# A linear-attention block and a SoLU block in one kernel: conversion order, the second group's keys, fetch order, and the place of state reads

## Chip, core and metric

The kernel runs on one core of a Trainium2 chip. The metric is its device time in microseconds, as the median of several runs. Before the change it is 368.37 us (three runs, 367.83 to 369.05).

## What is computed

Gated linear attention over 4 batches, 8 heads, 768 tokens and 48 channels, followed by a feed-forward block on the 3072 tokens of 384 channels (8 heads side by side):

```python
for t in range(S):
    state = alpha[:, :, t, :, None] * state + np.einsum('bhd,bhe->bhde', k[:, :, t], v[:, :, t])
    y[:, :, t] = np.einsum('bhd,bhde->bhe', q[:, :, t], state)
...
h = x @ w_in                                  # 384 -> 1024
solu = h * softmax(h)
ln = (solu - mean) / sqrt(var + 1e-06) * g_ln
return ln @ w_out                             # 1024 -> 384
```

The two weight matrices come as 64-bit floats; everything else is float32.

## The kernel before, in words

The 768 tokens are cut into G = 6 groups of 128 tokens in each of B = 4 batches, so a group is 512 tokens (T4). For each group there are two jobs. The attention job turns alpha, k and q so that channels lie on partitions, makes running products of alpha by a backward and a forward scan on VectorE (`scan_back`, `scan_on`, line 204), multiplies keys and queries by them, forms scores inside the chunk (`scores`, line 278), masks them (line 289), reads the carried state (`read_state`) and the values (`read_values`, both line 333) into x, and updates the state (`next_state`, line 371). The feed-forward job does eight blocks f of 128 hidden channels: `up_mm` (line 394, three products of 128 x 128 by 128 x 512), the exponential on ScalarE (line 408), the product h * e on VectorE (line 409), its square on ScalarE (line 412), then `down` (line 507, eight products of 128 x 128 by 128 x 385 for each of four token blocks), and `finish`, which normalises with sums that `array_sums` and `token_sums` gather on TensorE. Every float32 product is two matmul instructions in the trace, each with its own weight load.

The order of instructions on each engine is written out by hand; each engine works through its own queue in order, and a queue waits where its next instruction needs something. DMAs are issued from SyncE's queue (SP), in order too.

The stretch that the change touches most is the start. Group 0's attention is done first. Then group 0's up loop (`for f in range(FC)`, line 747) runs while the 64-bit weights arrive and are turned into float32 in eight pieces: pieces 0 to 3 are `w_in` (two blocks f each), pieces 4 to 7 are `w_out`. Each piece takes five VectorE steps, `bit(i, k)` with k = 0 to 4 (lines 616, 620, 624, 628, 630; 128 x 768 elements each, and each step needs the one before it). `fetch` brings raw pieces into slots of `room`, a buffer of six slots whose slots are also used for the hidden activations u; a fetch into a slot waits until the piece in it was converted and examined (`in_range`, ScalarE, lines 598 and 601). Pieces of `w_out` are then scaled by `g_ln` on ScalarE (`scaled`, line 637).

Behind the up loop (lines 773 to 844) stand, by hand: group 1's keys and queries, turned by TensorE against the identity (`turned`, line 164), the four `down` blocks of group 0, sums, the mean of `w_out` (`mean`, line 651 and 658), scans, `keys_back` (line 303, which turns the finished keys back for the state update), scores and masks of group 1, and group 1's state and value reads. From the third group on, keys, queries and alpha are turned by VectorE in 32 x 32 blocks (`firsts`, `lasts`, lines 179 and 182), and keys and queries are multiplied on GpSimd.

Last comes the main loop over g = 1 to 5 (line 922): group g's up blocks, with the down blocks of the group before between them, and group g + 1's attention in pieces that two tables name by step s: `first` for g = 1 and `usual` for g = 2, 3, 4. `head` comes ahead of the up block of step s, `behind` after it, `middle` ahead of the down block, `tail` after it. `attend` (line 863) turns the names into work. There, `lasts` stands for the queries' last 16 channels: turning, copying the decay's end (`ends_of_decay`), multiplying, and eight DMAs to `q64` (`move_lasts`); `firsts` is the same for the first 32 channels with four DMAs (`move_firsts`). `decay` multiplies the state on GpSimd by the ends that arrive in `q64`.

PSUM is handed out by tag: `ps_h` has two buffers for h, `ps_o` two for down, and `ps_a` has four single banks, a0 to a3, which scores, reads, turns and sums share.

## Time and profile before

| what | us |
|---|---|
| median of 3 runs | 368.37 |
| the profiled execution, its own time | 367.97 |
| its span, first to last instruction | 366.2 |
| PE busy in the span | 357.8 |
| VectorE busy | 245.0 |
| ScalarE busy | 146.4 |
| GpSimd busy | 132.2 |

By stretch (us of busy time):

| stretch | PE | VectorE | ScalarE | GpSimd | DMA share |
|---|---|---|---|---|---|
| 0 to 30 | 26.88 | 20.78 | 15.61 | 9.54 | 0.92 |
| 30 to 40 | 10.00 | 9.83 | 7.54 | 0.00 | 0.77 |
| 40 to 50 | 10.00 | 8.90 | 8.24 | 0.00 | 1.11 |
| 50 to 60 | 10.00 | 9.76 | 7.14 | 0.00 | 1.05 |
| 60 to 70 | 10.00 | 9.69 | 5.37 | 0.00 | 0.23 |
| 70 to 80 | 9.85 | 8.17 | 6.34 | 0.47 | 0.32 |
| 110 to 120 | 9.74 | 8.85 | 4.91 | 9.11 | 0.62 |
| 320 to 366 | 41.34 | 15.37 | 9.18 | 10.34 | 0.09 |

A line of the timeline gives the start in us, how long the run of like instructions took, engine, source line, operation, the tiles written and read, shapes and count; what stands in brackets is idle time before it and what ended that. Times in the trace count from the start of the span. A matmul's end is modelled and includes the way through the array, so the rate is read from starts.

### The profile page before, as it was taken

Reading aid. Unit: us, or ns where it says so; the run is one execution under the profiler, and the core shown is the slowest. Engines: PE = TensorE matmul, PEld = TensorE weight load, DVE = VectorE, ACT = ScalarE, POOL = GpSimd, SP = SyncE. Lnnn points to the kernel's source line nnn. Section 1 sums busy time; section 2 is a strip of 40 time slices with the busy share of each in tenths; the row PEclk is TensorE's granted clock in tenths of the full one; section 3 lists DMA queues with packets and bytes.
Section 4 is the critical chain, followed back from the end, with each engine's and each line's share of the span. In section 5 each row is a group of like instructions: output and inputs, shape, how many; then the busy total and the mean of one; then the engine's idle time right before and its main releaser. Section 6 shows DMA issues by size and latency. Waiting matters only on the chain. (4 is left out here: it accounts for less than half of the span.)

```text
span 366.2 us, 10036 instructions
## 1 busy us (share of the span) xinstructions
PE 357.8 (98%) x4341; PEld 215.0 (59%) x4341; DVE 245.0 (67%) x375; ACT 146.4 (40%) x260; POOL 132.2 (36%) x129
## 2 busy tenths in 40 slices
PE   8899999999999999999999999999999999999994
PEld 8784355666755566566575456475556565555552
DVE  0999989979998797936675935766946314345420
ACT  3647878182645262252521252431241132222110
POOL 7020000004449963774133764232773121233300
PEclk9999999999999999999999999999999999999999
DMA  9995995326196409463035354004041000000011
GB/s 180 183 338 152 204 309 124 88 67 159 50 234 141 109 21 180 85 152 94 21 92 112 83 121 126 3 25 88 21 107 55 0 25 0 24 21 22 23 47 51
DMA packets 72871, 36.06 MB, mean 98 GB/s; under 512 B 48232, under 2 KB 70000, under 8 KB 72816
## 3 DMA queue, kind: packets, MB, share of 16 engines
q1 hardware_dynamic: 71792, 34.39, 39.8%
q10 hardware_dynamic: 1024, 0.92, 0.8%
q8 instruction: 36, 0.59, 0.7%
q14 instruction: 19, 0.16, 0.2%
HBM read 25.30 MB, written 4.72 MB: 82 GB/s over the span
## 5 line engine op out<-in xcount | busy, mean ns | idle before, releaser
L507 PE MATMUL o<-w_out,room 128*128 128x385 f32 x384 | 134.0, 492 | 0.0
L394 PE MATMUL h<-x,w_in 128*128 128x512 f32 x288 | 131.7, 597 | 0.5 <-DVE g_col L642 0.5
L507 PEld LDWEIGHTS o<-w_out,room 128*128 128x128 f32 x384 | 71.0, 189 | 54.7 <-issue 13.1
L394 PEld LDWEIGHTS h<-x,w_in 128*128 128x128 f32 x288 | 53.2, 189 | 58.6 <-issue 48.5
L409 DVE TENSOR_TENSOR room<-h,e 128x512 f32<-128x512 f32 x40 | 27.5, 689 | 72.9 <-ACT e L408 72.9
L408 ACT ACTIVATE e<-h 128x512 f32<-128x512 f32 x40 | 24.0, 599 | 100.2 <-PE h L394 100.2
L427 POOL TENSOR_TENSOR p<-p,e 128x512 f32<-128x512 f32 x30 | 43.7, 1458 | 20.0 <-ACT e L408 19.9
L412 ACT ACTIVATE u<-room 128x512 f32<-128x512 f32 x40 | 25.2, 630 | 38.3 <-DVE room L409 38.3
L546 POOL TENSOR_TENSOR r<-sums,mhalf 128x1 f32<-128x1 f32 x20 | 14.8, 741 | 69.7 <-DVE sums L537 69.4
L289 DVE TENSOR_TENSOR sT<-a,mask 128x512 f32<-128x512 f32 x43 | 26.7, 681 | 8.0 <-PE a L278 7.9
L204 DVE TENSOR_TENSOR_SCAN hT<-aT,unit 128x516 f32<-128x516 f32 x18 | 24.4, 1399 | 7.6 <-ACT aT L703 7.5
L204 DVE TENSOR_TENSOR_SCAN aT<-aT,seed 128x516 f32<-128x516 f32 x18 | 27.4, 1551 | 0.2
L225 POOL TENSOR_TENSOR kT<-kT,hT 128x1024 f32<-128x1024 f32 (+1 forms) x8 | 14.2, 1800 | 32.7 <-DVE kT L179 32.7
L427 DVE TENSOR_TENSOR p<-p,u 128x512 f32<-128x512 f32 x30 | 22.5, 749 | 5.1 <-ACT u L412 5.1
L278 PEld LDWEIGHTS a<-qv,kT 32*128 32x128 f32 x704 | 21.4, 186 | 7.0 <-issue 2.6
L278 PE MATMUL a<-qv,kT 32*128 32x128 f32 x704 | 23.9, 278 | 0.4 <-POOL qv L253 0.3
L212 POOL COPY fend<-hT 128x12 f32<-128x12 f32 x6 | 3.1, 509 | 55.9 <-DVE hT L204 55.9
L333 PE MATMUL y<-sT,vn 128*32 128x128 f32 x768 | 22.6, 273 | 0.2 <-DVE sT L289 0.2
L333 PEld LDWEIGHTS y<-sT,vn 128*32 128x32 f32 x768 | 20.7, 110 | 1.6 <-issue 1.0
L196 ACT ACTIVATE sq<-an,mone 128x1536 uint8<-128x1536 f32 x12 | 18.9, 1572 | 0.2
L548 ACT ACTIVATE o_sb<-o,r 128x384 f32<-128x384 f32 x16 | 9.3, 582 | 18.5 <-POOL r L546 18.5
L261 POOL TENSOR_TENSOR state<-state,lot 128x384 f32<-128x384 f32 x10 | 8.8, 903 | 13.1 <-DMA lot<-qv 13.1
(148 smaller groups left out, 374.3 us busy)
## 6 DMA issues: line engine op xcount, KB each, us to landing
vn<-in_v_dram SPq DMA_DIRECT2D x24, 192.0 KB, 4.7
an<-in_alpha_dram SPq DMA_DIRECT2D x20, 192.0 KB, 4.1
out_dram<-o_sb SPq DMA_DIRECT2D x20, 192.0 KB, 1.9
room<-in_moe_w_out_dram SPq DMA_DIRECT2D x8, 384.0 KB, 5.5
kn<-in_k_dram SPq DMA_DIRECT2D x16, 192.0 KB, 5.6
qn<-in_q_dram SPq DMA_DIRECT2D x16, 192.0 KB, 4.1
lot<-qe SPq DMA_DIRECT2D x40, 64.5 KB, 2.1
lot<-qv SPq DMA_DIRECT2D x20, 129.0 KB, 2.4
```

What stands on the lines that cost most here:

```text
L196: nc.scalar.activation(out=sq, in_=x, func=AF.Relu, scale=sign, bias=mone, accum_out=over[:, g, i : i + 1])
L204: nc.vector.tensor_tensor_scan(out=o, data0=a, data1=s, initial=1.0, op0=ALU.mult, op1=ALU.add)
L278: nc.tensor.matmul(a[b][:, i], lhsT=kT[quarter(b), kb], rhs=qv[quarter(b), qb, 0:P], start=not last and not i, stop=bool(last), tile_posit ...
L289: nc.vector.tensor_tensor(out=sT[:, b, half * NP : half * NP + NP], in0=a[b], in1=mask[:, None, :].to_broadcast([P, NP, P]), op=ALU.mult,)
L333: nc.tensor.matmul(y_bank(b)[quarter(r), a], lhsT=lhsT, rhs=rhs, start=(b, r) not in begun, stop=stop, tile_position=(row, 32 * r), skip_g ...
L394: nc.tensor.matmul(h, lhsT=w_in[:, a, f * P : (f + 1) * P], rhs=d["x"][:, a].rearrange("p b t -> p (b t)"), start=(a == 0), stop=(a == KC ...
L408: nc.scalar.activation(out=e, in_=h, func=AF.Exp)
L409: nc.vector.tensor_tensor(out=u, in0=h, in1=e, op=ALU.mult)
L412: nc.scalar.activation(out=u2, in_=u, func=AF.Square)
L427: eng.tensor_tensor(out=p, in0=d[0][i] if f == 1 else p, in1=d[f][i], op=ALU.add)
L507: nc.tensor.matmul(d["o"][:, 0 : DM + 1], lhsT=u_of(g, f)[:, b * P : b * P + P], rhs=w_out[:, f], start=(f == 0), stop=(f == FC - 1), skip ...
L546: nc.gpsimd.tensor_tensor(out=r, in0=s[:, 3:4], in1=mhalf, op=ALU.pow)
```

## The change

What it does, in the order of the diff's parts:

- The copies of the decay's end for group 2 (the third) are done by ScalarE and not by GpSimd.
- In group 0, up blocks f = 2 to 7 are computed in two halves of 256 columns; the first thirty down steps (blocks n = 0 to 2 and f = 0 to 5 of n = 3) in two halves of 192 and 193 columns.
- The last three small operations of `token_sums(0)` are put off until after the second half of group 1's masks.
- A fetch of two pieces lays them in one slot each, and not interleaved.
- Piece 0 is converted in two halves (one up block each); from piece 1 on, the steps of one piece and of the next alternate. As many steps as before come ahead of the up loop; their distribution over f differs.
- k of group 1 is loaded in the plain layout, and VectorE turns it (`keys_T(1)`); TensorE's turn of it and ScalarE's copy of its ends fall away. The load of k for group 2 stands behind that turn.
- Fetches of pieces 5 and 6 go to f = 1 and f = 3, ahead of alpha's load, which moves from f = 0 to f = 3.
- Behind the up loop, `down(0, 0)` precedes the array sums, and all of q's turns stand together ahead of the mean. PSUM tags are dealt out anew. Scans and key multiplications alternate differently.
- For group 2, q is turned ahead of the main loop, and two of the three forward scans move from there into steps 0 and 1; `lasts` moves from step 2 to step 1.
- In groups 4 and 5 (the last two), the first half of the state read moves from step 6 to step 7, directly ahead of the second half.

```diff
-    def ends_of_decay():
-        nc.gpsimd.tensor_copy(out=qe[:, :, P:SW], in_=h4[:, H:NB, 1:2])
-        nc.gpsimd.tensor_copy(out=qv[:, 0:H, P:SW], in_=h4[:, 0:H, 1:2])
+    def ends_of_decay(copy=nc.gpsimd.tensor_copy):
+        copy(out=qe[:, :, P:SW], in_=h4[:, H:NB, 1:2])
+        copy(out=qv[:, 0:H, P:SW], in_=h4[:, 0:H, 1:2])
...
+        w = T4 if g or f < 2 else T4 // 2
         for a in range(KC):
-            nc.tensor.matmul(
-                h, lhsT=w_in[:, a, f * P : (f + 1) * P], rhs=d["x"][:, a].rearrange("p b t -> p (b t)"),
-                start=(a == 0), stop=(a == KC - 1),
-            )
+            x = d["x"][:, a].rearrange("p b t -> p (b t)")
+            for c in range(0, T4, w):
+                nc.tensor.matmul(
+                    h[:, c : c + w], lhsT=w_in[:, a, f * P : (f + 1) * P], rhs=x[:, c : c + w],
+                    start=not a and not c, stop=(a == KC - 1), skip_group_check=True,
+                )
...
         tt = work.tile([P, B, 2, 32], FP, name="cols")
         nc.vector.transpose(out=tt.rearrange("p b i t -> p (b i t)"), in_=t.rearrange("p b i t -> p (b i t)"))
         s = sums[:, g * B : g * B + B]
-        nc.vector.tensor_copy(out=s[:, :, 1:3], in_=tt[:, :, :, 0])
-        sq = small.tile([P, B], FP, name="sq")
...
-        d["s"] = small.tile([P, B], FP, name="s")
-        nc.vector.scalar_tensor_tensor(
...
+        def rest():
+            nc.vector.tensor_copy(out=s[:, :, 1:3], in_=tt[:, :, :, 0])
...
+            nc.vector.tensor_tensor(out=sq, in0=s[:, :, 1], in1=s[:, :, 1], op=ALU.mult)
+            d["s"] = small.tile([P, B], FP, name="s")
...
+        if g:
+            rest()
+        else:
+            d["rest"] = rest
...
+            w = DM // 2 if n * FC + f < 30 else DM + 1
+            for c in range(0, DM, w):
+                e = DM + 1 if c + w >= DM else c + w
+                nc.tensor.matmul(
+                    d["o"][:, c:e], lhsT=u_of(g, f)[:, b * P : b * P + P], rhs=w_out[:, f, c:e], start=not f and not c,
+                    stop=(f == FC - 1), skip_group_check=True,
+                )
...
-        raw = room[:, 1536 * slot : 1536 * (slot + n)].bitcast(U32).rearrange("p (c f w) -> p c f w", f=w, w=2)
+        raw = room[:, 1536 * slot : 1536 * (slot + n)].bitcast(U32)
+        raw = raw.rearrange("p (m c f w) -> p c m f w", m=n, f=w // n, w=2)
...
-                nc.sync.dma_start(out=raw[rows, c].rearrange("p f w -> p (f w)"), in_=src.bitcast(U32))
+                nc.sync.dma_start(
+                    out=raw[rows, c].rearrange("p m f w -> p m (f w)"),
+                    in_=src.bitcast(U32).rearrange("p (m x) -> p m x", m=n),
+                )
...
-            raws[i + m] = raw[:, :, w // n * m : w // n * (m + 1)]
+            raws[i + m] = raw[:, :, m]
...
+    def bit(i, k, part=None):
...
+        dst = place(i)
         top, low = made[i]
+        if part is not None:
+            lo, hi, top, low, dst = (x[:, :, P * part : P * part + P] for x in (lo, hi, top, low, dst))
...
-        m = ps_h.tile([P, 512], FP, tag="h", name="sums")[:, 0:DM]
+        m = ps_a.tile([P, 512], FP, tag="a3", name="sums")[:, 0:DM]
...
-    bits(0)
+    bits((0, k, part) for k, part in ((0, 0), (0, 1), (1, 0), (1, 1), (2, 0), (2, 1), (3, 0), (4, 0), (3, 1), (4, 1)))
     read_values(0)
     gains()
     keys_back(0)
     in_range(0)
-    bits(1)
...
+    steps = [(1, 0), (1, 1)]
+    for i in range(1, 8):
+        steps += [(i, 2), (i + 1, 0), (i, 3), (i + 1, 1), (i, 4)]
+    steps = [x for x in steps if x[0] < 8]
+
+    def convert(n):
+        bits(steps[:n])
+        del steps[:n]
+
+    convert(5)
+    checks = {0: [(2, 0)], 1: [(2, 1)], 2: [(3, 0)], 3: [(3, 1)], 4: [(4, 0), (4, 1)], 5: [(1, 0), (1, 1)]}
...
+        if f == FC - 1:
+            scaled(5)
...
     for f in range(FC):
         up_mm(0, f)
         if f == 4:
...
         up_act(0, f, lambda: check(f))
-        for _ in range((4, 2, 3, 3, 3, 3, 3, 9)[f]):
...
+        convert((5, 2, 3, 2, 5, 4, 2, 7)[f])
         if f == 0:
             next_state(0)
             fetch(4, 3)
-            load_first(k, kn, 1)
+            load(k, kn, 1)
             load_first(q, qn, 1)
+        elif f == 1:
+            fetch(5, 1)
+        elif f == 3:
+            fetch(6, 2)
             load(alpha, an, 1)
-        elif f == 2:
-            ends_k = ends_of(kn, "e")
-        elif f == 3:
-            fetch(5, 1)
-            fetch(6, 2)
             ends_q = ends_of(qn, "u2")
         elif f == 5:
             fetch(7, 3)
             load_v(1)
         elif f == 6:
             scaled(4)
-    tk = three("tp_k", [(ps_a, "a2"), (ps_a, "a3"), (ps_h, "h")])
-    turned(kn, ends_k, tk)
+    down(0, 0)
+    array_sums(0, 1)
+    scaled(6)
+    scaled(7)
+    down(1, 0)
+    keys_T(1)
     load(k, kn, 2)
-    array_sums(0, 1)
-    scaled(5)
-    down(0, 0)
-    scaled(6)
+    token_sums(0)
     alpha_over(1)
-    token_sums(0)
     alpha_T(1)
     load(alpha, an, 2)
-    down(1, 0)
-    scaled(7)
-    tq = three("tp_q", [(ps_a, "a0"), (ps_a, "a1")])
-    turned(qn, ends_q, tq, range(H))
-    for i in range(3):
-        scan_back(1, i)
-        part = slice(NP * i, NP * i + NP)
-        nc.vector.tensor_tensor(out=kT[:, part], in0=tk[i], in1=hk[:, part], op=ALU.mult)
+    tq = three("tp_q", [(ps_a, "a0"), (ps_h, "h"), (ps_a, "a2")])
+    turned(qn, ends_q, tq)
+    for i in (0, 1, None, 2):
+        if i is not None:
+            scan_back(1, i)
+        for j in {1: (0,), None: (1,), 2: (2,)}.get(i, ()):
+            part = slice(NP * j, NP * j + NP)
+            nc.vector.tensor_tensor(out=kT[:, part], in0=kT[:, part], in1=hk[:, part], op=ALU.mult)
     inverses(1)
     mean(0)
     down(0, 1, (0, 1))
     mean(1)
     down(0, 1, (2, 3))
     hold(0)
-    tq += three("tp_q2", [(ps_h, "h")])
-    turned(qn, ends_q, tq, range(H, NB))
     down(1, 1)
     hold(1)
-    keys_back(1, three("tp", [(ps_a, "a2"), (ps_a, "a3"), (ps_h, "h")]))
+    keys_back(1, three("tp", [(ps_a, "a1"), (ps_a, "a3"), (ps_h, "h")]))
     scan_on(1, 2)
     nc.vector.tensor_tensor(out=qe[:, :, 0:P], in0=tq[2], in1=aT[:, H:NB, 1:SW], op=ALU.mult)
     apart()
@@ -821,6 +844,7 @@
     down(2, 1)
     scores(1, 1)
     masked(1)
+    gr[0]["rest"]()
     finish(0)
     finish(1)
     finish(2)
@@ -839,24 +863,24 @@
     keys(2)
     load(k, kn, 3)
     down(3, 1, (2, 3))
-    scan_on(2, 2)
-    scan_on(2, 0)
+    lasts(qn, qe[:, :, 0:P])
+    firsts(qn, qv[:, 0:H, 0:P])
 
 
 
...
-        middle={6: "begin read0", 7: "read1 values"},
...
+        middle={6: "begin", 7: "read1 values"},
...
         behind={
-            0: "v", 1: "on1", 2: "lasts firsts", 3: "apart", 4: "scores0 masked0", 5: "scores1 masked1 decay",
+            0: "v on2", 1: "on0 lasts", 2: "on1 firsts", 3: "apart", 4: "scores0 masked0", 5: "scores1 masked1 decay",
...
-        tail={6: "begin read0"},
+        tail={6: "begin"},
...
-            if what == "on2":
+            if what == "on2" and a > 2:
                 inverses(a)
...
-            lasts(qn, qe[:, :, 0:P])
-            ends_of_decay()
+            if a > 2:
+                lasts(qn, qe[:, :, 0:P])
+            ends_of_decay(nc.gpsimd.tensor_copy if a > 2 else nc.scalar.copy)
...
-            firsts(qn, qv[:, 0:H, 0:P])
+            if a > 2:
+                firsts(qn, qv[:, 0:H, 0:P])
...
-        elif what[:4] == "read":
-            read_state(int(what[4]))
+            if a < 4:
+                read_state(0)
+        elif what == "read1":
+            if a > 3:
+                read_state(0)
+            read_state(1)
```

More of the change, by code (lines that the diff above doesn't have):

```diff
@@ L468, in token_sums @@
         s = sums[:, g * B : g * B + B]
-        nc.vector.tensor_copy(out=s[:, :, 1:3], in_=tt[:, :, :, 0])
-        sq = small.tile([P, B], FP, name="sq")
-        nc.vector.tensor_tensor(out=sq, in0=s[:, :, 1], in1=s[:, :, 1], op=ALU.mult)
-        d["s"] = small.tile([P, B], FP, name="s")
-        nc.vector.scalar_tensor_tensor(
-            out=d["s"], in0=sq, scalar=1e-6 * DFF, in1=s[:, :, 2], op0=ALU.mult, op1=ALU.add
-        )
+        def rest():
+            nc.vector.tensor_copy(out=s[:, :, 1:3], in_=tt[:, :, :, 0])
+            sq = small.tile([P, B], FP, name="sq")
+            nc.vector.tensor_tensor(out=sq, in0=s[:, :, 1], in1=s[:, :, 1], op=ALU.mult)
+            d["s"] = small.tile([P, B], FP, name="s")
+            nc.vector.scalar_tensor_tensor(
+                out=d["s"], in0=sq, scalar=1e-6 * DFF, in1=s[:, :, 2], op0=ALU.mult, op1=ALU.add
+            )
[3 more added lines that the diff above has]
+            d["rest"] = rest
     def last_norm():
@@ L506, in down @@
         for f in (half * HF + i for i in part):
-            nc.tensor.matmul(
-                d["o"][:, 0 : DM + 1], lhsT=u_of(g, f)[:, b * P : b * P + P], rhs=w_out[:, f], start=(f == 0),
-                stop=(f == FC - 1), skip_group_check=True,
-            )
+            w = DM // 2 if n * FC + f < 30 else DM + 1
[5 more added lines that the diff above has]
+                )
     def hold(n):
@@ L577, in fetch @@
             if float64:
-                nc.sync.dma_start(out=raw[rows, c].rearrange("p f w -> p (f w)"), in_=src.bitcast(U32))
+                nc.sync.dma_start(
+                    out=raw[rows, c].rearrange("p m f w -> p m (f w)"),
+                    in_=src.bitcast(U32).rearrange("p (m x) -> p m x", m=n),
+                )
             else:
@@ L601, in in_range, with bits @@
             nc.scalar.activation(out=sq, in_=sq, func=AF.Exp, scale=-(2.0**24), accum_out=far[:, i, 1:2])
-    def bits(i, steps=range(5)):
-        for k in steps if float64 else ():
-            bit(i, k)
-    def bit(i, k):
+    def bits(steps):
+        for x in steps if float64 else ():
+            bit(*x)
+    def bit(i, k, part=None):
         lo, hi = raws[i][:, :, :, 0], raws[i][:, :, :, 1]
-        if k == 0:
+        if k == 0 and not part:
             made[i] = [
@@ L629, in bit @@
         else:
-            nc.vector.tensor_tensor(out=place(i), in0=low, in1=top, op=ALU.add)
+            nc.vector.tensor_tensor(out=dst, in0=low, in1=top, op=ALU.add)
     def scaled(i):
@@ L737, in fast_path @@
     in_range(0)
-    bits(1)
-    steps = [(i, step) for i in range(2, 8) for step in range(5)]
-    checks = {0: [(2, 0)], 1: [(2, 1)], 2: [(3, 0)], 3: [(3, 1)], 4: [(1, 0), (1, 1)], 5: [(4, 0), (4, 1)]}
+    steps = [(1, 0), (1, 1)]
[7 more added lines that the diff above has]
+    checks = {0: [(2, 0)], 1: [(2, 1)], 2: [(3, 0)], 3: [(3, 1)], 4: [(4, 0), (4, 1)], 5: [(1, 0), (1, 1)]}
     def check(f):
@@ L751, in fast_path @@
         up_act(0, f, lambda: check(f))
-        for _ in range((4, 2, 3, 3, 3, 3, 3, 9)[f]):
-            step = steps.pop(0)
-            if float64:
-                bit(*step)
+        convert((5, 2, 3, 2, 5, 4, 2, 7)[f])
         if f == 0:
```

## Prediction

> **What bounds the kernel now.** I read the page's first table, then the groups, then PE's waits, then the timeline of three stretches, because a share of busy time does not say whether PE works at its rate.
>
> ```profile
> span 366.2 us, 10036 instructions
> PE 357.8 (98%) x4341; PEld 215.0 (59%) x4341; DVE 245.0 (67%) x375; ACT 146.4 (40%) x260; POOL 132.2 (36%) x129
> L507 PE MATMUL o<-w_out,room 128*128 128x385 f32 x384 | 134.0, 492 | 0.0
> L394 PE MATMUL h<-x,w_in 128*128 128x512 f32 x288 | 131.7, 597 | 0.5 <-DVE g_col L642 0.5
> ```
>
> PE has work for 98% of the span. The timeline of a late stretch tells at what rate (start, duration, and the count of a run of equal matmuls):
>
> ```profile
> 305.47 2.74 PE L394 MATMUL h<-x,w_in 128*128 128x512 f32 x6
> 308.04 2.75 PE L507 MATMUL o<-w_out,room 128*128 128x385 f32 x8
> 310.63 2.74 PE L394 MATMUL h<-x,w_in 128*128 128x512 f32 x6
> ```
>
> From start to start, six up matmuls take 2.57 us, 429 ns each; eight down matmuls take 2.59, 323 each. The starts are evenly spaced over nearly the whole trace, so **TensorE is the bound**, and a change pays by matmuls it removes, by switches between full-array and tiled blocks, or by gaps. Gaps exist only early. VectorE is the engine closest behind, in the stretch where it turns 64-bit weights into float32 (lines 614 to 630):
>
> ```profile
> 38.72 0.68 DVE L409 TENSOR_TENSOR room<-h,sT 128x512 f32<-128x512 f32 x1
> 39.32 0.95 DVE L620 SCALAR_TENSOR_TENSOR lot<-room,lot 128x768 uint32<-128x768 uint32 x1
> 40.30 0.56 DVE L624 TENSOR_SCALAR lot<-lot 128x768 uint32<-128x768 uint32 x1
> 40.90 0.96 DVE L628 SCALAR_TENSOR_TENSOR lot<-room,lot 128x768 f32<-128x768 uint32 x1
> 41.77 0.68 DVE L409 TENSOR_TENSOR room<-h,sT 128x512 f32<-128x512 f32 x1
> ```
>
> There is no idle time here. A step that needs the one before it (40.30 after 39.32 + 0.95) starts 0.03 us after its end; one that doesn't (39.32 after 38.72 + 0.68) starts 0.08 before. So dependence costs 0.11 us. How close VectorE comes to PE is read from this:
>
> ```profile
> 71.83 0.69 DVE L791 TENSOR_TENSOR kT<-tp_k,hT 128x512 f32<-128x512 f32 x1
> 73.88 1.47 PE L303 MATMUL tp<-ident,kT 128*128 128x128 f32 x12
> 77.76 0.69 DVE L811 TENSOR_TENSOR qv<-tp_q,aT 128x512 f32<-128x512 f32 x1
> 77.87 2.69 PE L278 MATMUL a<-qv,kT 32*128 32x128 f32 x64
> ```
>
> Group 1's keys are done at 72.52, and PE takes them at 73.88: VectorE has 1.3 us in hand. At 77.87 PE has begun its scores, but bank a1 still holds queries that L811 reads until 78.45: from start to the next block (80.49) it takes 2.62, where the same block at 83.28 takes 2.00.
>
> [...] L616 takes 0.94 on pieces 2 and 3, which lie interleaved in one fetch, and 0.55 on pieces that lie alone.
>
> **The change part by part.** I walked PE, VectorE and ScalarE through their queues from 23.9 us with the durations of these rows; on the order of before the walk gives 72.57 for the keys (trace 72.52) and 73.72 for PE's keys_back (73.88).
>
> *Keys by VectorE.* The 96 matmuls of the keys (start 52.90, next block 55.55) go: **-2.65 on PE**. ScalarE's copy of their ends (0.60) goes. VectorE gets a transpose of 128x1024 and one of 128x512 (L179 and L182, 2.12 and 1.10 for group 2's keys at 94.63 and 96.61, less 0.2 of overlap): +3.0. The multiply by hk costs the same with its source in SBUF (0.69 in L791; L427 is 0.69 as well).
>
> *Conversions side by side.* Outside piece 0, 22 steps start behind their own predecessor now and 4 afterwards: 18 x 0.115 = -2.1. Pieces 2 and 3 in slots of their own: 2 x 0.39 = -0.8. Piece 0 in halves: 384 columns lie between the rows for 512 (0.68) and 768 (0.957), 0.55 each[...]. Its ten halves end 0.16 later than the five now, but the half that f = 0 needs ends at 27.3 in place of 28.24, so PE's wait at 28.39 goes: **-0.46**. If PE waited for both halves this would be lost; the wait below would take it up.
>
> *The rest of the norm sums put off:* three operations, 0.2 each, -0.6 before the keys; they come back behind the masks at 86, 13 us ahead of the next product that PE waits for. Scans and multiplies in alternating order: -0.5.
>
> *Order of PE:* down(0,0) before the array sums; token sums, all query turns and mean in a row. A down between two tiled blocks takes 2.81, beside one 2.70, beside none 2.59, and a tiled block some 0.14 for its start. Two blocks fewer: **-0.45**. But down(0,0) comes right behind the last up, while ScalarE has yet to scale w_out (piece 4): Square(6) waits for VectorE's product at 51.0, then two scalings of 0.51: PE waits about 1.0.
>
> *Split matmuls:* 36 in up, 60 in down more, 2.5 ns each: **+0.24**.
>
> *DMAs on SP:* k by four plain loads (768-byte rows, issue 0.45 each, as alpha's) and not two of 192-byte rows (4.6 us of issue), so q and what is behind it start earlier; fetch(5) goes ahead at f = 1, behind piece 2's last step (38.4); fetch(6) behind piece 3 (43.2), then alpha, used by ScalarE at 61 and VectorE at 63.5, some 15 us later; fetch(7) and v behind. k for group 2 waits on SP for VectorE's keys turn (63.2), with alpha behind it, which had to wait until 66.8 anyway. Nothing for the end, while pieces land in 4 to 5 us.
>
> *The sum at keys_back.* VectorE: -2.1 - 0.8 + 0.16 + 3.0 - 0.6 - 0.5, and 0.2 more of idle time (it waits 0.9 for the last exponential, behind the scalings), in all -0.6: keys at 71.95, PE at 72.1. PE alone would be there at 73.88 - 0.46 - 2.65 - 0.45 + 0.17 = 70.5. So **1.6 us of PE's saving turns into a wait for VectorE**, part at down(0,0), part at keys_back, and keys_back is 1.8 earlier. Behind it the queries' first part is ready at 75.9 and PE arrives at 76.1; the banks of scores now hold queries read earlier (a0, a2), so **-0.6**: -2.4. The state reads of group 1 wait for the last mask until 86.0, and PE comes there at 85.8 (88.07 now).
>
> *Group 2's queries sooner.* Both transposes before the up loop, two scans into it; POOL multiplies their last part at about 103.5 in place of 109.8, the eight DMAs and the four behind on SP start 6 us earlier, decay's wait for them goes. The decay ends go from POOL (1.13 + 0.72) to ScalarE, which has room (40%). VectorE's product of f = 0 comes at 99.2, PE needs it at 101.4. PE now waits 0.26 at 113.12, and its blocks at 107.55, 113.12 and 118.09 are 0.6 over their pure time; I take **-0.3** (bounds 0 and -0.6).
>
> *Reads in a row,* groups 4 and 5 (the last two) alone: an up before the lone read takes 2.77 and not 2.57, the down behind 2.69 and not 2.59, and the second read's start of some 0.1 goes: 0.4 each, **-0.8**. The decay is long done.
>
> Sum: -1.8 - 0.6 + 0.07 (28 more split downs) - 0.3 - 0.8 = **-3.4**. The profiled execution took 367.97, its span 366.17: it becomes 364.6. The median of three is 0.4 above that execution: **365.0**.
>
> **Rivals.** *No new wait* (0.16): VectorE's chain is 1.6 shorter than I walk it, because the last exponential comes sooner (0.9 in question) [...]. For: it had slack before. Against: the walk meets the trace to 0.05. It gives 365.0 - 1.6 = 363.4. *Pieces late* (0.15): fetch 5 was issued at 42.93 and its piece began at 49.55, 6.6 us, with DMA full from 40 to 50 (share 1.11). At that pace piece 5 is 0.7 and piece 6 1.0 late, all 1.7 of it on VectorE's chain: 366.7. Against: 192-byte rows of k are gone and alpha is moved out of the way. *The weight loads of the halves show* (0.07): a half needs the same load as the whole. Were x of each of 96 loads bare, PE gains 3.4 - 96x; from 35 ns on the kernel is slower, and with the whole 189 it is +14.7, 383.1. Against: 109 ns from start to start with a load each, under 162 and 215.
>
> **How the numbers follow.** My case 0.62, on its own 363.8 to 366.1. The range takes in late pieces and most of the no-wait case: 363.2 to 367.1. A measurement of this kernel tells 0.3% (1.1 us) from no change, the limit being 367.3: faster 0.62 + 0.16 + 0.10 = 0.88, within 0.07 (most of it late pieces), slower 0.05 (bare loads).
>
> **What would show it.** No keys among PE's turns of group 1, and up matmuls of 256 at 216 ns; no wait at the first up; PE waits of together about 1.6 at down(0,0) and keys_back; VectorE's conversions done at 60 and not 62.8; L616 at 0.55 for every whole piece; scores at 76.1 with 2.0 us; a read of 128 tiled matmuls before the values in groups 4 and 5. Wrong if halves start more than 220 ns apart, or if VectorE idles for w_out pieces.

## The result, and the profile after

The changed kernel takes **367.58 us** (median of 22 runs, 366.17 to 369.73), the kernel before 368.40 in 22 runs beside it (367.83 to 369.05): a ratio of 0.9972, 95% interval 0.9961 to 0.9983. Forecast were 365.0 and a range of 363.2 to 367.1. The sign was right, the size was not: of the 3.4 us that were forecast, 0.8 were gained. The profiled execution took 367.89, its span is 366.1.

From the page of the kernel after, the lines that answer to those of before, and the line of the DMA queue named "instruction" (packets, MB, share):

```profile
span 366.1 us, 10052 instructions
PE 355.5 (97%) x4341; PEld 228.7 (62%) x4341; DVE 243.4 (66%) x382; ACT 146.4 (40%) x261; POOL 131.0 (36%) x127
q8 instruction: 36, 0.59, 0.7%
```

PE is busy 2.3 us less, as wanted: the 96 matmuls of the keys are gone. The count of matmuls is the same, since the splits add 96. But the span is only 0.1 shorter, so PE stands still 2.2 us more. Where it does so, PE's waits say (engine, tile, line, what was waited for; total us, times, longest):

```profile
PE o L519 <- ACT w_out L656: 1.2, 1, 1.2
...
PE h L397 <- issue: 0.8, 1, 0.8
PE a L278 <- DVE qv L834: 0.8, 1, 0.8
...
PE y L333 <- issue: 0.5, 1, 0.5
```

The same view of the kernel before has none of these four. The first was forecast at 1.0. "Issue" means that the engine waited for nothing the profile shows. PE's timeline has both such waits inside runs of equal matmuls (start, duration, count, and the idle time ahead in brackets):

```profile
22.95 0.65 PE L333 MATMUL y<-sT,vn 128*32 128x128 f32 x14 [0.20 <-DVE sT L289]
24.12 3.04 PE L333 MATMUL y<-sT,vn 128*32 128x128 f32 x102 [0.53 <-issue]
...
31.29 1.57 PE L371 MATMUL kv<-vn,kg 128*32 128x48 f32 x128
32.78 2.41 PE L397 MATMUL h<-x,w_in 128*128 128x512 f32 x5
36.03 1.24 PE L397 MATMUL h<-x,w_in 128*128 128x512 f32 x4 [0.83 <-issue]
```

Before, both runs go through without a stop (in the second, the up block's six matmuls and four of the next):

```profile
22.85 3.47 PE L333 MATMUL y<-sT,vn 128*32 128x128 f32 x116 [0.20 <-DVE sT L289]
...
32.63 4.56 PE L394 MATMUL h<-x,w_in 128*128 128x512 f32 x10
```

Now the second up block stops after five of its six matmuls, though the sixth needs only the x and w_in that the fifth had. A bracket counts from the modelled end of the matmul ahead; from start to start the stop costs 1.0 us, and the one ahead of 24.12 costs 0.8. Farther on, VectorE's end of the keys and of the queries' first product, and PE's blocks beside them:

```profile
73.62 0.69 DVE L816 TENSOR_TENSOR kT<-kT,hT 128x512 f32<-128x512 f32 x1
73.56 1.47 PE L303 MATMUL tp<-ident,kT 128*128 128x128 f32 x12
77.69 0.69 DVE L834 TENSOR_TENSOR qv<-tp_q,aT 128x512 f32<-128x512 f32 x1
78.44 0.82 PE L278 MATMUL a<-qv,kT 32*128 32x128 f32 x18 [0.78 <-DVE qv L834]
```

The keys are done at 74.31 where 71.95 was forecast (72.52 before), and the scores start at 78.44 where 76.1 was forecast (77.87 before). The reads of group 1, after and then before:

```profile
88.06 1.23 PE L333 MATMUL y<-lot,state 64*32 64x128 f32 x64
89.23 1.57 PE L519 MATMUL o<-w_out,room 128*128 128x192 f32 x8
90.73 1.64 PE L333 MATMUL y<-lot,state 64*32 64x128 f32 x64
92.30 4.08 PE L333 MATMUL y<-sT,vn 128*32 128x128 f32 x128
96.30 1.56 PE L519 MATMUL o<-w_out,room 128*128 128x385 f32 x4
97.70 0.59 PE L397 MATMUL h<-x,w_in 128*128 128x512 f32 x1
```

```profile
90.71 1.16 PE L333 MATMUL y<-lot,state 64*32 64x128 f32 x64
91.79 3.70 PE L333 MATMUL y<-sT,vn 128*32 128x128 f32 x128
...
96.83 1.45 PE L394 MATMUL h<-x,w_in 128*128 128x512 f32 x3
```

Two equal reads now take 1.23 and 1.64, and the values 4.08 in place of 3.70 before. So group 1's up loop starts at 97.70, 0.87 *later* than before (96.83); behind that the change gains 0.95. Nearly all that is missing was lost ahead of 98 us.

### The profile page after: what moved, and what is told of

Same layout as the page of the kernel before. It is cut to its first block, busy times and chain, and to the rows that moved or that the text cites. A ratio compares the mean times of both kernels' runs of the same rounds, so it can differ in the third digit from the quotient of the medians.

```text
span 366.1 us, 10052 instructions
## 1 busy us (share of the span) xinstructions
PE 355.5 (97%) x4341; PEld 228.7 (62%) x4341; DVE 243.4 (66%) x382; ACT 146.4 (40%) x261; POOL 131.0 (36%) x127
## 5 line engine op out<-in xcount | busy, mean ns | idle before, releaser
L519 PE MATMUL o<-w_out,room 128*128 128x385 f32 (+2 forms) x444 | 133.9, 447 | 1.2 <-ACT w_out L656 1.2
L397 PE MATMUL h<-x,w_in 128*128 128x512 f32 (+1 forms) x324 | 131.9, 549 | 0.8 <-issue 0.8
L519 PEld LDWEIGHTS o<-w_out,room 128*128 128x128 f32 x444 | 79.9, 189 | 51.0 <-issue 13.4
L397 PEld LDWEIGHTS h<-x,w_in 128*128 128x128 f32 x324 | 60.1, 189 | 53.1 <-issue 42.4
L225 POOL TENSOR_TENSOR kT<-kT,hT 128x1024 f32<-128x1024 f32 (+1 forms) x8 | 13.3, 1685 | 33.6 <-DVE kT L179 33.6
L204 DVE TENSOR_TENSOR_SCAN aT<-aT,seed 128x516 f32<-128x516 f32 x18 | 24.8, 1408 | 0.2
L430 DVE TENSOR_TENSOR p<-p,u 128x512 f32<-128x512 f32 x30 | 21.3, 709 | 5.1 <-ACT u L415 5.1
L333 PE MATMUL y<-sT,vn 128*32 128x128 f32 x768 | 23.4, 274 | 0.7 <-issue 0.5
```

Source lines behind the costliest of these rows:

```text
L204: nc.vector.tensor_tensor_scan(out=o, data0=a, data1=s, initial=1.0, op0=ALU.mult, op1=ALU.add)
L333: nc.tensor.matmul(y_bank(b)[quarter(r), a], lhsT=lhsT, rhs=rhs, start=(b, r) not in begun, stop=stop, tile_position=(row, 32 * r), skip_g ...
L397: nc.tensor.matmul(h[:, c : c + w], lhsT=w_in[:, a, f * P : (f + 1) * P], rhs=x[:, c : c + w], start=not a and not c, stop=(a == KC - 1), ...
L430: eng.tensor_tensor(out=p, in0=d[0][i] if f == 1 else p, in1=d[f][i], op=ALU.add)
L519: nc.tensor.matmul(d["o"][:, c:e], lhsT=u_of(g, f)[:, b * P : b * P + P], rhs=w_out[:, f, c:e], start=not f and not c, stop=(f == FC - 1), ...
```

## Theories

**Late program blocks.** The queue named "instruction" moved 0.59 MB in 36 packets, 16.4 KB each; the trace has 8,740 records of PE (weight loads, matmuls and its waits), some 243 to a packet. Counted from 0 through these records, each gap marked "issue" above stands ahead of record 193 plus a multiple of 256, and PE goes on 1.3 to 1.6 us behind the end of one of these packets. I call 256 such records a block and the place between two blocks a boundary. In the table, the second column is when PE entered the block ahead of the boundary, the fourth when it would have gone on without a stop (times from the trace's records):

| kernel, boundary ahead of PE record | block before entered | packet | PE was ready | PE went on |
|---|---|---|---|---|
| after, 961 | 18.52 | 21.81 to 22.75 | 23.35 | 24.12 |
| after, 1473 | 31.33 | 33.52 to 34.46 | 35.0 | 36.03 |
| after, 2753 | 88.10 | 89.08 to 90.56 | 91.62 | 91.99 |
| before, 961 | 18.51 | 20.99 to 21.93 | 23.25 | 23.25 |
| before, 1473 | 31.18 | 32.44 to 33.36 | 34.88 | 34.88 |

Before, the same packets came 0.8 and 1.1 us earlier, just in time (they ended 1.3 and 1.5 us ahead of the need). All 17 traces of this document together have 35 gaps of PE over 60 ns that are marked "issue". Every one stands at such a boundary (ahead of record 193 or 194 plus a multiple of 256), and every one ends 1.3 to 1.7 us behind a packet.

A boundary need not show. Of the 36 packets, 33 belong to boundaries inside PE's records. In before and in after alike, PE's first record behind such a boundary comes 1.3 us or more behind the end of the packet (1.31 and 1.38 at the least), and before has no gap at any. At the 35 gaps PE could go on 3.3 to 6.2 us behind the entry of the block ahead, and had used that block up in 1.5 to 5.0. Next state's 128 small matmuls with their loads (31.29 to 32.78) use up a block in 1.5 us. From the packet's start to PE's going on, the three gaps of after took 2.3, 2.5 and 2.9 us.

**VectorE's chain.** From 50 to 78 us VectorE is the second bound, by a chain of work that I walked too short. The two theories can both hold.

**Rivals:** operands that the profile doesn't name, or matmuls that cost more than their columns.

## Experiments

Ratios are to the kernel before, with 95% intervals.

**1. The changed kernel again, and its DMAs moved (four runs).** Hold: the fetch of pieces 2 and 3 of the weights waits until the first half of group 0's masks is done. K late: group 1's k is loaded behind alpha. Both: the two edits together.

```diff
-    fetch(2, 1, 2)                      # hold, and both
+        if half == 0:                   # in the mask loop
+            for m in (1, 2):
+                nc.gpsimd.memset(slots[m][:, 0:1536:512], 0.0)
+            fetch(2, 1, 2)
-            load(k, kn, 1)              # k late, and both: from f == 0
+            load(k, kn, 1)              # to f == 3, behind alpha
```

> The changed kernel once more, nothing edited. Theory (late program blocks): PE's two unexplained gaps, in the reading of values (0.7 us at 23.3 of the trace) and inside up f = 1 (1.0 us at 34.6), lie 512 instructions apart and each ends 1.4 to 1.6 us after a 16 KB packet of the program queue has landed; they come back at the same instruction, with a size that varies with how late that packet starts (0 to 1.5 us each), and the total lies at 366 to 369. Rival (operands): the gaps come from data or from a wait that the profile does not tell; they come back at the same instruction with about the same size, whatever the program packet does.

> The fetch of weight pieces 2 and 3 is held until the first half of group 0's masks is done (22.4 us), by a small write to their slots; it was issued at about 20. Theory (late program blocks): DMA is less full from 20 to 22.4, the program packet that PE asks for at 18.5 starts by 20.5 and not at 21.8, and the gap in the values (0.7) goes; the gap in f = 1 stays at 0.5 to 1.3. Total 0.3 to 0.8 below the changed kernel. Rival (operands): the gap in the values stays. A danger for both: pieces 2 and 3 land late (needed at 30.9), then VectorE waits for them.

> The load of group 1's k goes from f = 0 to f = 3, behind alpha; q's stays at f = 0. Theory (late program blocks): DMA has less in hand at 31.3, when PE asks for the program packet that it needs at 34.6; the packet starts by 32.5 and not at 33.5, and the gap in f = 1 shrinks from 1.0 to 0 to 0.4; the one in the values stays. VectorE's chain starts earlier by as much, the scores of group 1 too. Total 0.5 to 1.2 below the changed kernel. Rival (operands): the gap in f = 1 stays, the total within 0.3.

> Both: pieces 2 and 3 held, and k's load behind alpha's. Theory (late program blocks): both gaps go, 1.7 us on PE ahead of f = 2, so that VectorE's chain and the scores of group 1 come 1.5 to 1.8 earlier; total 365.3 to 366.3, what was forecast less one microsecond at most. Rival (operands): no change beyond 0.3. Second rival (VectorE's chain is too long by itself): the gaps go, but the scores still start at 78 and the total stays at 367.

Again: 367.14 (0.9975, 0.9963 to 0.9987). Hold: 368.01 (0.9995, 0.9982 to 1.0008). K late: 367.68 (0.9984, 0.9969 to 0.9999). Both: 367.93 (1.0007, 0.9986 to 1.0029). No time moved clearly, and the gains forecast for the three edits (0.3 to 0.8, 0.5 to 1.2, and a time of 365.3 to 366.3 for both) did not come; the traces tell more. The same kernel again has no gap at record 961 (its packet came at 20.87), 0.8 us at 1473 and 1.5 at 2753: the gaps come and go, the places stay. Hold took all three gaps away, and the sixth up block began at 44.33 in place of 46.17. But then VectorE waited 1.4 us at first steps of pieces, and PE stood 2.1 us ahead of the first down; 0.5 us behind that wait the granted clock of PE fell to 0.5 for 3.4 us, and the first 16 half matmuls of down took 4.5 us where the changed kernel took 3.0. K late took the gap at 1473 away (packet at 31.30). Both together had all three, one packet again at 21.84. So every gap lies on a block boundary behind a late packet, but I could not order a packet's time by what I moved.

**2. Boundaries moved by the warm-up (four runs).** These kernels change the number of PE instructions ahead of everything else, which by the theory moves every later boundary by as many instructions: fewer by 48 in after and in before (warm-up products four times as wide), more by 8 in before, fewer by 8 in after (`warm(12)` for `warm(14)`). The three edits, in this order:

```diff
-        for i in range(n):
-            nc.tensor.matmul(t[:, 0:P], lhsT=ones, rhs=ones, start=True, stop=True)
+        for w in (4,) * (n // 4) + (1,) * (n % 4):
+            nc.tensor.matmul(
+                t[:, 0:w], lhsT=ones, rhs=ones[:, None, :].to_broadcast([P, w, P]), start=True, stop=True
+            )
```

```diff
+        for i in range(2 if n == 14 else 0):
+            nc.tensor.matmul(t[0:32, 0:32], lhsT=ones[:, 0:32], rhs=ones[:, 0:32], start=True, stop=True)
```

```diff
-    warm(14)
+    warm(12)
```

> The changed kernel with the 18 warm-up products of 128 columns given to TensorE as 8 (four of 512 columns for every four of 128): the same columns, 48 fewer PE instructions ahead of everything else, nothing else touched. Theory late blocks (PE's program comes in blocks of 256 instructions, fetched by one packet when the block before is entered): every later block boundary comes 48 instructions later in the work. The boundary that lay in the second up block (34.6) moves to about 39.6, with 8.8 us from the trigger of its fetch to its need in place of 3.7; the one at 91.6 moves to 92.7 with 3.9 in place of 3.4. So no gap in PE between 30 and 40, the sixth up block begins at 44.3 to 45.2 and not at 46.2, the queries of group 2 (97.70) at 96.0 to 96.9, and the whole takes 0.8 to 1.5 us less than the changed kernel. One at 19.5 or 23.8 with 4.3 us can still be late. Theory late operands (PE waits in the up loop for something that the profile does not name): the gap stays at 34.6, time within 0.3 of the changed kernel.

> The kernel before with the same edit of the warm-up products (48 fewer PE instructions, the same columns). Its boundaries had no gap, and the moved ones have 4.1 us or more except one at 92.4 with 3.9. Late blocks: within 0.5 us of before, either sign. Late operands: no change. If this one gains as much as the changed kernel does from the same edit, the gain is of the warm-up itself and not of the boundaries.

> The kernel before with two more warm-up products of 32 columns each at the start (8 more PE instructions, some 0.2 us while PE waits for data). Late blocks: the boundary at 34.9 moves to 33.2, into the dense run of next state's matmuls, and only 2.0 us lie between the trigger of its fetch and its need, where packet and way to PE take 2.4 at least: a gap of 0.5 to 3 us opens at 33.2, before any in the rest, and the kernel becomes 0.5 to 2.5 us slower than before. Late operands: nothing at all, under 0.2 us.

> The changed kernel with 12 warm-up products in place of 14: 8 fewer PE instructions ahead of everything. Late blocks: each boundary 8 instructions later; the one at 34.6 with some 0.5 us more between entry and need, the one at 91.6 with less and that at 95.7 with more: 0 to 0.6 us less than the changed kernel, with gaps in other places. Otherwise no change.

After with 48 fewer: 368.87 (1.0028, 1.0009 to 1.0046). Before with 48 fewer: 368.91 (1.0019, 1.0004 to 1.0034). Before with 8 more: 369.31 (1.0032, 1.0019 to 1.0045). After with 8 fewer: 367.60 (0.998, 0.9968 to 0.9993). The gaps did move to the new boundaries (after with 48 fewer: none from 30 to 40, but idle times of 1.1 us ahead of 25.41, 0.4 ahead of 92.70 and 1.2 ahead of 240.81), and PE still went on 1.3 to 1.6 behind a packet. An unnamed operand would have kept its place in the work, so that rival falls. My *numbers* missed: I forecast a gain of 0.8 to 1.5 for the first and got a loss against the changed kernel, 1.3 by the medians and 2.1 by the ratios. Before with 48 fewer was to stay within 0.5 and lost 0.7, with a gap of 0.6 ahead of 24.70. In before with 8 more the gap at 33.2 hardly opened (0.1) and others did, 0.5 ahead of 23.95 and 0.2 ahead of 141.72. I had priced the boundaries that I moved away from and not all that I moved to. After with 8 fewer lost both early gaps, but has one of 0.8 ahead of 91.83 and two waits for GpSimd's state near 123 us, 0.8 together; its time is that of the changed kernel. That before loses 0.7 and 1.1 us by moves in either direction fits boundaries that lay well; what the warm-up edits cost of themselves was not measured apart.

**3. The splits: none, 39 more in halves, 32 in thirds (three runs).** All three keep every column.

```diff
-        w = T4 if g or f < 2 else T4 // 2
+        w = T4                                                        # none
-            w = DM // 2 if n * FC + f < 30 else DM + 1
+            w = DM + 1                                                # none
+            w = DM // 2 if n * FC + f < 69 else DM + 1                # 39 more halves
+            w = DM // 2 if n * FC + f < 30 else DM // 3 if n * FC + f < 62 else DM + 1   # thirds
```

> The changed kernel with up and down matmuls whole as before (192 fewer PE instructions from the third up block on). By my sum the splits cost 96 x 2.5 ns = 0.24 us. Late blocks: the boundary at 34.6 lies ahead of the first split, so its gap stays; those behind move by up to 192 instructions, away from the reads of group 1 (91.6) to about 91.4 with 6.2 us and 94.7 with 3.2, so that gap is gone or smaller. In all -0.2 to -0.8 against the changed kernel, or +0.3 if the one at 94.7 is late. Rival, bare weight loads: the splits cost 35 ns each and more, so it becomes 3 us faster.

> The changed kernel with 39 more down matmuls split in two (those of group 1, behind 113 us): 156 more PE instructions there, no more columns. By the sum of the prediction 39 x 2 x 2.5 ns = 0.20 us, so 367.4 to 367.8, and any rival without a program fetch says the same. Theory late blocks: from there on the boundaries fall at other places, among them into the runs of 128 tiled matmuls of next state and of the reads (near 236, 246 and 290 us), with 1.8 to 2.8 us from the entry to the need in place of 3.5 and more: gaps marked as issue at two to four of them, 0.5 to 2 us each, and the whole 2 to 4 us slower than the changed kernel.

> The changed kernel with 32 down matmuls (the last two of group 0 and 30 of group 1) split in three: 256 more PE instructions, exactly one block, so that the block boundaries behind the last of them (some 180 us) lie in the work where they lie in the changed kernel. Theory late blocks: though it adds 100 instructions more than the kernel with 39 split in two, it loses little: 64 x 2 x 2.5 ns = 0.32 us, and between 130 and 180, where the boundaries are still on their way, at most one gap more of 0.5 to 3 us; behind 185 the run of PE is that of the changed kernel within 0.3. In all 0.3 to 2.5 us above the changed kernel. Rival, splits or more instructions cost as such (9 us for 39 halves, 0.23 each): 64 more matmuls make it 12 to 15 us slower, spread beyond 185.

None: 368.85 (1.0018, 1.0008 to 1.0029). The halves were forecast 2 to 4 us above the changed kernel. **39 halves: 377.63 (1.0255, 1.0212 to 1.0297). Thirds: 367.52 (0.9991, 0.9978 to 1.0004).** This pair settles it. 78 more matmul instructions cost 10 us; 128 more, which with their loads are exactly one block, cost 0.7 by the ratios (0.32 by the estimate of 2.5 ns each; the intervals of this kernel and the changed one just overlap), and nothing by the medians. So matmuls that cost more as such are not the cause. PE's timeline of the kernel with 39 halves, all five places behind 113 us with a wait for "issue", and the block behind the first:

```profile
141.54 0.22 PE L465 MATMUL rows<-p,ones 128*32 128x64 f32 x1 [2.92 <-issue]
141.69 4.55 PE L519 MATMUL o<-w_out,room 128*128 128x192 f32 x16
...
191.87 1.50 PE L333 MATMUL y<-sT,vn 128*32 128x128 f32 x42 [1.28 <-issue]
246.90 2.60 PE L333 MATMUL y<-sT,vn 128*32 128x128 f32 x85 [0.39 <-issue]
258.37 0.31 PE L465 MATMUL rows<-p,ones 128*32 128x64 f32 x4 [1.57 <-issue]
303.32 3.05 PE L333 MATMUL y<-sT,vn 128*32 128x128 f32 x104 [1.12 <-issue]
```

and the first of these places with thirds:

```profile
137.81 0.64 PE L465 MATMUL rows<-p,ones 128*32 128x64 f32 x32
138.38 2.94 PE L519 MATMUL o<-w_out,room 128*128 128x128 f32 x24
```

With halves, a block began at 136.94 and was used up at 138.40, 1.5 us later; the packet behind it ran from 138.57 to 139.82, and the last one of 32 equal matmuls began at 141.54. With thirds the 32 run through. From group 1's up loop to the last matmul, halves take 10.3 us more than the changed kernel. At the five places stand 8.5 of it (start to start). Most of the rest is the clock: from 142.63, 1.1 us behind the longest stop, the granted clock of PE is 0.5 for 3.4 us; nine halves of the down block there start 320 ns apart where the changed kernel's start 164 apart, and the stretch loses some 1.7 us. The last 0.2 is left for the splits themselves. From up block to up block, the delay against the changed kernel grows by 4.8, 1.7, 0.8, 1.8 and 1.1 us in the five stretches that hold these places, and between them by those 0.2 alone.

Without splits, PE reached group 1's up loop at 95.84 in the profiled execution, earlier than any other with the whole work, and then lost 0.7, 0.3 and 0.6 (start to start) at boundaries at 186.3, 241.1 and 294.9: I expected a gain of 0.2 to 0.8 and got 1.3 us more time by the medians, 1.7 by the ratios. By these traces the 96 splits are worth their cost (0.24 us by the prediction's estimate, some 0.3 by the 2.6 and 4 ns measured below) because they put the boundaries of the later groups back where they were before the keys' 96 matmuls left.

**4. VectorE's chain (four runs).** Scaled early moves `scaled(4)` from f = 6 to f = 5. Less VectorE leaves step 3 out for pieces 5 to 7, so the low halves of these weights stay unscaled: it measures what VectorE's time is worth and is no kernel to use. Two products and one product of the keys go to GpSimd in the last two runs, both with scaled early; with one, the third scan stands ahead of the products.

```diff
+            scaled(4)                                                 # scaled early, at f == 5
-        elif f == 6:
-            scaled(4)
...
-        elif k == 3:
+        elif k == 3 and i < 5:                                        # less VectorE
...
-            nc.vector.tensor_tensor(out=kT[:, part], in0=kT[:, part], in1=hk[:, part], op=ALU.mult)
+            (nc.vector if j == 2 else nc.gpsimd).tensor_tensor(...)   # two products
...
+    for i in range(3):                                                # one product
+        scan_back(1, i)
+    for j in (1, 0, 2):
+        part = slice(NP * j, NP * j + NP)
+        (nc.gpsimd if j == 1 else nc.vector).tensor_tensor(...)
```

> The changed kernel with the scaling of w_out's first converted piece put one up block earlier in ScalarE's order. PE's wait of 1.2 us ahead of the first down goes. Theory VectorE is the bound between 50 and 78: its chain to the keys and queries of group 1 stays where it is, PE waits 2.0 to 2.2 instead of 1.0 for the queries' product ahead of the scores, the first read of group 1 begins within 0.3 of before this edit, and the time is the same within 0.3. Rival, each wait counts for itself: the first read 1.2 earlier, time 1.2 less.

> The changed kernel without the fourth step (a product of 0.96 us) in the conversion of the last three weight pieces: the low halves of these weights are left unscaled, so part of the result is not the reference's. 2.9 us less for VectorE, nothing else. Theory VectorE is the bound between 50 and 78: the wait at the first down shrinks by some 0.8, the one ahead of the scores (1.0) goes, the first read of group 1 begins 1.6 to 2.2 earlier (at 85.0 to 86.5) and the time falls by 1.2 to 2.2. Rival, only the program fetch matters: 0.3 at most.

> The changed kernel with w_out's first scaling one block earlier and with two of the three products of group 1's keys (0.69 us each) given to GpSimd, which is idle there from 24.7 to 72.6. Theory VectorE is the bound between 50 and 78: its chain to the queries' product is 1.3 shorter, PE's wait ahead of the scores (1.0) goes, the first read of group 1 begins at 85.8 to 86.4, and the time is 0.8 to 1.4 below the changed kernel, so 366.2 to 366.8. If GpSimd's products take over 1.6 each, the keys are late instead and nothing is gained. Block boundaries lie in the same places as in the changed kernel.

> As the run with w_out's first scaling one block earlier, and one of the three products of group 1's keys on GpSimd, but with VectorE's third scan put ahead of the products, so that the scan has no product of GpSimd ahead of it to wait for (in the run with two products on GpSimd it stood still for 2.5 us). GpSimd's product takes 1.16 there. Theory VectorE is the bound between 50 and 78: the queries' product is 0.7 earlier from the start of the up loop, PE's wait ahead of the scores falls from 1.0 to 0.3, the first read of group 1 comes at 86.0 to 86.9, and the time is 0.4 to 1.2 below the changed kernel: 366.4 to 367.2. Rival, the chain is bound elsewhere: as the run with the scaling alone (367.0) or above.

Scaled early: 367.00 (0.9968, 0.9952 to 0.9983). **Less VectorE: 365.11 (0.9915, 0.9898 to 0.9932).** Two products on GpSimd: 368.01 (0.9987, 0.9975 to 0.9998). One product there: 366.38 (0.9956, 0.9931 to 0.998). With less VectorE, PE does not stand ahead of the scores (no bracket), and they take 2.07 us:

```profile
76.08 2.07 PE L278 MATMUL a<-qv,kT 32*128 32x128 f32 x64
```

The scores start at 76.08 and the first read at 85.70: that is where the prediction had them (76.1 and 85.8). It takes 2.9 us off VectorE to get there, and it brings 2.5 us against the changed kernel by the medians, 2.1 by the ratios. So VectorE does bound that stretch. With scaled early, the wait at the first down fell from 1.2 to 0.5, and the one ahead of the scores stayed at 0.8, where 2.0 to 2.2 was forecast. The first read came at 87.05 (87.04 in the changed kernel's second trace), and the time is within the uncertainty of the changed kernel's. But PE lost 0.5 us more at late blocks ahead of this stretch than in that second trace, so what the wait itself was worth isn't shown. Two products on GpSimd were forecast at 366.2 to 366.8 and failed in a way of their own: VectorE stands still beside them.

```profile
72.59 1.23 DVE L204 TENSOR_TENSOR_SCAN hT<-aT,unit 128x516 f32<-128x516 f32 x1 [2.50 <-POOL kT L815]
```

```profile
70.24 2.32 POOL L815 TENSOR_TENSOR kT<-kT,hT 128x512 f32<-128x512 f32 x2 [45.94 <-DVE hT L204]
```

The profile puts the scan's wait down to GpSimd's products, which read another part of hT; what holds it isn't settled. With the scan ahead and one product, no wait is left ahead of the scores, but PE waits 1.0 for GpSimd's product instead, and the first read comes at 88.10 where 86.0 to 86.9 was forecast, in a profiled execution that also stood 2.0 us at two late blocks. By its median it is the fastest kernel here with the whole result, 0.9956 of before; its seven runs reach from 365.10 to 368.18, so that it beats the changed kernel isn't settled.

## Why the prediction was wrong, step by step

*Steps that held.* From the sixth up block to keys_back the time fell from 28.90 (44.98 to 73.88) to 27.39, of which 1.27 is the wait at down(0,0): 2.78 less of work, against 2.65 + 0.45 - 0.17 = 2.93 forecast. Halves of up start 215.8 ns apart on the mean and whole ones 429.0, so a split costs 2.6 there; halves of down start 164 apart and whole ones 324, some 4 a split. The prediction's 2.5 was an estimate; transposes of 128 columns (L303) at 109.1 and up matmuls of 512 at 429.0 differ by 0.833 ns a column and leave 2.4 beside the columns. A weight load of up or down shows 186 to 193 ns (the prediction's 189), yet halves with a load each start 216 and 164 apart: loads don't show here. (The 109 ns of a transpose, which has a load of 138 to 143, are its own columns and these 2.4; they bound what shows of a load and do not measure it.) A whole piece's first step takes 0.55 to 0.60 for every piece, and the other halves of piece 0 take 0.53 to 0.56 for 0.55, though 384 columns lie below the two rows that the prediction set them between. The wait at down(0,0) is 1.2 for 1.0, by the cause named. VectorE waited 0.3 us for pieces in all, so "pieces late" did not come. Group 2's queries: 97.70 to the down at 131.83 takes 34.13 for 34.76, so 0.6 gained for 0.3 (its bound). Reads in a row:

```profile
236.94 2.04 PE L333 MATMUL y<-lot,state 64*32 64x128 f32 x128
238.91 3.70 PE L333 MATMUL y<-sT,vn 128*32 128x128 f32 x128
```

There is one read of 128 in place of two of 64. The step takes 13.54 for 13.95 in group 4 and 13.78 for 13.95 in group 5: 0.6 gained for 0.8. Behind 98 us the sum was 1.1 and 0.95 came.

*The step that failed* is "The sum at keys_back" and with it "Gaps exist only early": PE was walked as if its next matmul ran as soon as its operands were there, so the time at block boundaries was put at nothing; the page's instruction queue was not read at all. And VectorE's chain, which that sum did price, was walked 1.0 us too short. By the sum group 1's up loop would have started at 96.83 - 2.33 = 94.50; it started at 97.70. The 3.2 us are three terms, worked out from the changed kernel with 8 warm-up instructions fewer, whose profiled execution has no gap ahead of 91 us:

| term | how | us |
|---|---|---|
| program blocks at 24 and 35 us, handed on by VectorE | scores at 78.44 here, 77.13 there | 1.3 |
| VectorE's chain walked too short | scores at 77.13 there, 76.1 forecast | 1.0 |
| program blocks in the reads of group 1 | first read to up loop 9.64, before 8.76 | 0.9 |

These are single executions, so the sizes are theirs. The first term is not PE's alone: when up blocks are late, the exponentials are, VectorE's products h * e wait for them (3.0 us between 23 and 63 in the changed kernel, 1.7 with 8 instructions fewer), and the conversions end at 62.59 in place of 61.27. Of the 1.8 us that the two gaps cost PE, 1.3 were still there at the scores. The gap of 0.8 ahead of 24.12 also ate the head wait's 0.46: in the seven traces of the changed kernel and its variants without a gap there, the first up block came at 27.75 to 28.04, close to the forecast 27.93.

The second is a term that was mis-sized. Conversions end at 61.27 without gaps; "done at 60" was forecast. I took 0.2 more idle time on VectorE than before's 0.9 (0.5 for an exponential, 0.4 for a piece). It is 1.74 in two places: 0.85 where the last exponential stands behind the scalings (I had that one) and 0.89 ahead of 44.37, for an exponential that ScalarE began only behind PE's array sums (I had not). That is 0.65 more than I took. The halves of piece 0's first and third steps took 0.51 (two first steps, behind GpSimd's mask product) and 0.40 (two third steps), together another 0.4 over what I took, an estimate that no row of before showed.

The forecast wait of 0.6 at keys_back (1.6 less the 1.0 at the first down) did not show: PE came late itself, at 73.56, and turns the keys by parts, the last of which VectorE finished at 74.31 while PE was at work. It stood ahead of the scores instead (0.8), so VectorE's bound was in the right stretch and named at the wrong block. Of the rivals, "no new wait" had VectorE's chain 1.6 shorter; it was 1.0 longer.

*Not settled:* what sets a packet's start. Ahead of the 35 gaps it came 0.8 to 3.9 us behind the entry of the block before, longest (3.0 to 3.9) at the boundary near 24 us, where DMA is full (share 0.83 and 1.03 in the two stretches from 18.5 to 24), and differently from one execution to the next. It fits that the changed kernel's 22 runs spread over 3.6 us and the 22 of before beside them over 1.2. How much of the median's 2.6 us is program and how much VectorE can be told for profiled executions only; less VectorE bounds the second at 2.5.

## What to carry to other kernels

Where PE runs many small matmuls, count its instructions, loads included: 256 of them were a block here, and a stretch that uses up a block in less time than the next one needs to come (at the gaps here 1.5 to 5.0 us against 3.3 to 6.2, from the block's entry) can stall at the boundary. Such a stall was marked as "issue" inside a run of equal matmuls, and 48 or 8 instructions fewer or more ahead of everything moved the boundaries behind them; splitting matmuls, at 2.6 to 4 ns a split, put them back here. And a gain on the busiest engine was worth here what the second one left (2.9 us off VectorE brought 2.5): walk that one with its own waits for each block, not with a sum of idle time.

## What was not expected of the hardware

- 39 more splits, 0.2 us of work by the sum, made the kernel 10 us slower, and 32 products in thirds (64 more) 0.7 by the ratios; the longest stall at a block boundary was 2.92 us.
- A stop can cost more than itself. Behind PE's two longest waits in these traces (2.92 us with 39 halves, 2.10 with Hold) the granted clock was 0.5 for 3.4 us, and matmuls took twice as long (halves of down 320 ns from start to start and not 164, with 39 halves). Behind the next longest (1.60 and 1.57) it stayed at 1.0. What a wait between these does, no run here shows.
- At the 35 gaps PE went on 1.3 to 1.7 us behind the end of a packet, and a packet took 0.9 to 1.8. In the 17 traces no packet began more than 45 PE records ahead of the entry of the block before (the last two packets of each trace left out, which belong to places behind the kernel's last PE record), so in these traces a packet's lead was one block, no more.
- GpSimd's product of 128 x 512 took 1.16 us while VectorE stood still, and 2.08 beside VectorE's products and scan; that scan took 1.96 in place of 1.23:

```profile
72.59 2.08 POOL L814 TENSOR_TENSOR kT<-kT,hT 128x512 f32<-128x512 f32 x1 [48.48 <-DVE hT L204]
```
